# Rearranging K with VectorE block transposes in an attention backward for one query row: a new layout, new loads, a new order

## The chip, the cores and the metric

One core of a Trainium2 chip. The metric is the device time of one execution in microseconds (us). A run more than 1.5% above the fastest of its kernel is called slow and left out of comparisons. Ratios are the mean time of one kernel's fast runs over that of the other's of the same rounds on the same chip (the rounds ran on several chips, each with the kernel before beside the others), so they are not quite the ratio of the medians quoted beside them.

## The reference

```python
B, H, Sq, Skv, Dh = 1, 32, 1, 8192, 128           # bf16
def fwd(q, k, v):
    scores = einsum('bhqd,bhkd->bhqk', q, k) * Dh ** -0.5
    return einsum('bhqk,bhkd->bhqd', softmax(scores), v)
# returns (out, dq, dk, dv) for a given grad_out
```

For each of 32 heads one query row meets 8192 rows of K and V, 2.1 MB each. dK and dV are outer products, 2.1 MB each. So a head moves 8.39 MB and computes little on it: 268 MB in all.

## The kernel before

A head is two tiles of 128 partitions x 64 rows x 128 columns in SBUF, the on-chip memory that transfers write to; the tensor engine's results come out in another one, PSUM. The scores q.K and dp = dO.V contract over the columns, so the tensor engine (PE) transposes both tiles in 128x128 blocks, ScalarE (ACT) copies the result out of PSUM, and 64 narrow products (one column each) for K and 64 for V follow. VectorE (DVE) writes dK and dV as outer products. SyncE (SP) issues all transfers on one queue.

```python
def load(h):                                      # and load_v(h) the same
    Kt[h] = kvpool.tile([P, NT, D], BF16, tag="K", name="Kt")
    nc.sync.dma_start(Kt[h][:], k[0, h].rearrange("(p n) d -> p n d", p=P))
...
def transposes(h, which, c):                      # 4 of these for K, 4 for V
    T_ps = psT.tile([P, CH, P], BF16, tag="T", name="T_ps")
    for i in range(CH):                           # CH = 16
        nc.tensor.transpose(T_ps[:, i, :], Xt[:, c * CH + i, :], ident[:])
    nc.scalar.copy(X.rearrange("p c s -> p (c s)").bitcast(F32), ...)
...
def store(h, G, dst, part):                       # two stores of 1 MB for dK, two for dV
    nc.sync.dma_start(dst[0, h].rearrange("(p n) d -> p n d", p=P)[:, part * L:(part + 1) * L, :],
                      G[:, part * L:(part + 1) * L, :])
```

Of the kernel before, what the change touches and what calls it, by code (L numbers as in the profile page):

```python
# [8 lines left out]
ACT = mybir.ActivationFunctionType  # L9
ALU = mybir.AluOpType  # L10
AX = mybir.AxisListType
BF16 = mybir.dt.bfloat16
F32 = mybir.dt.float32
PSUM = bass.MemoryType.PSUM

CH = 16
R = 4
KV_BUFS = 3
AHEAD = 2
NST = 2  # L20


@with_exitstack
def kernel(
# [11 lines left out]
    nc = tc.nc  # L36
# [5 lines left out]
    assert NCH == 4  # L42
# [3 lines left out]
    kvpool = ctx.enter_context(tc.tile_pool(name="kv", bufs=KV_BUFS))  # L46
# [6 lines left out]
    Kt, Vt = {}, {}  # L53

    def load(h):
        Kt[h] = kvpool.tile([P, NT, D], BF16, tag="K", name="Kt")
        nc.sync.dma_start(Kt[h][:], k[0, h].rearrange("(p n) d -> p n d", p=P))

    def load_v(h):
        Vt[h] = kvpool.tile([P, NT, D], BF16, tag="V", name="Vt")  # L60
        nc.sync.dma_start(Vt[h][:], v[0, h].rearrange("(p n) d -> p n d", p=P))
# [4 lines left out]
    for h in range(AHEAD):  # L66
        load(h)
        load_v(h)
# [6 lines left out]
    nc.vector.memset(ones_f[:], 1.0)  # L75

    qT = consts.tile([P, H], BF16)
    doT = consts.tile([P, H], BF16)
    for i, colsT in ((0, qT), (1, doT)):
        tp = psT.tile([P, CH, P], BF16, tag="T")  # L80
        nc.tensor.transpose(tp[:, 0, 0:H], rows[:, i, :], ident[0:H, 0:H])
        nc.vector.tensor_copy(colsT[:], tp[:, 0, 0:H])

    o_allT = consts.tile([P, H], BF16)
    dq_allT = consts.tile([P, H], BF16)
# [4 lines left out]
    st = {}  # L90
    XT = {}

    def transposes(h, which, c):
        Xt = Kt[h] if which == "K" else Vt[h]
        T_ps = psT.tile([P, CH, P], BF16, tag="T", name="T_ps")
        for i in range(CH):
            nc.tensor.transpose(T_ps[:, i, :], Xt[:, c * CH + i, :], ident[:])  # L97
        X = tpool.tile([P, CH, P], BF16, tag="XT", name="XT_sb")
        nc.scalar.copy(X.rearrange("p c s -> p (c s)").bitcast(F32),  # L99
                       T_ps.rearrange("p c s -> p (c s)").bitcast(F32))  # L100
        XT[which, c] = X

    def scores(h, which, c):
        X = XT.pop((which, c))
        out_cols, vecT = (st[h]["s"], qT) if which == "K" else (st[h]["dp"], doT)
        for i in range(CH):
            n = c * CH + i
            nc.tensor.matmul(out_cols[:, n:n + 1], lhsT=X[:, i, :], rhs=vecT[:, h:h + 1],  # L108
                             start=True, stop=True, skip_group_check=True)

    def contract(Xt, rep, out_col):
        for n in range(NT):
            nc.tensor.matmul(out_col, lhsT=Xt[:, n, :], rhs=rep[:, n, 0:1],  # L113
                             start=(n == 0), stop=(n == NT - 1), skip_group_check=True)
# [8 lines left out]

    def store(h, G, dst, part):
        L = NT // NST
        nc.sync.dma_start(dst[0, h].rearrange("(p n) d -> p n d", p=P)[:, part * L:(part + 1) * L, :],
                            G[:, part * L:(part + 1) * L, :])

    def ds_of(h):
        x = st[h]  # L130
        nc.tensor.matmul(x["m"][:, 1:2], lhsT=ones_f[:], rhs=x["pd"][:], start=True, stop=True,  # L131
                         skip_group_check=True)
        pdt = small.tile([P, 1], F32, tag="pdt")
        nc.vector.tensor_copy(pdt[:], x["m"][:, 1:2])
        rep = small.tile([P, NT, R], BF16, tag="dsrep", name="ds_rep")
        nc.vector.scalar_tensor_tensor(
            out=rep[:], in0=x["dp"][:, 0:NT].unsqueeze(2).to_broadcast([P, NT, R]), scalar=pdt[:],
            in1=x["p_s"][:].unsqueeze(2).to_broadcast([P, NT, R]), op0=ALU.subtract, op1=ALU.mult)
        x["ds"] = rep

    def dq_of(h):
        x = st[h]
        contract(Kt[h], x["ds"], x["o"][:, 1:2])
        nc.scalar.copy(dq_allT[:, h:h + 1], x["o"][:, 1:2])  # L144

    def dk_outer(h):
        x = st[h]
        G = gpool.tile([P, NT, D], BF16, tag="g0", name="G0")
        for r in range(4):
            outer_part(G, x["ds"], x["qd"][:, 0, :], r)  # L150
            if r % (4 // NST) == 4 // NST - 1:
                store(h, G, out_2, r // (4 // NST))

    for h in range(H + 1):
        if h < H:
            x = st[h] = {}
            x["s"] = psS.tile([P, 512], F32, tag="s", name="s_ps")
            transposes(h, "K", 0)
        if h > 0:
            ds_of(h - 1)  # L160
        if h < H:
            transposes(h, "K", 1)
            scores(h, "K", 0)
            transposes(h, "K", 2)
        if h > 0:
            dq_of(h - 1)
            if h - 1 + KV_BUFS < H:
                load_v(h - 1 + KV_BUFS)
                load(h - 1 + KV_BUFS)
            dk_outer(h - 1)  # L170
        elif AHEAD < KV_BUFS:
            load(AHEAD)
            load_v(AHEAD)
        if h == H:
            break
        scores(h, "K", 1)
        transposes(h, "K", 3)
        scores(h, "K", 2)
        x["dp"] = psS.tile([P, 512], F32, tag="dp", name="dp_ps")
        transposes(h, "V", 0)  # L180
        scores(h, "K", 3)
        mx = small.tile([P, 1], F32, tag="mx")
        nc.vector.reduce_max(mx[:], x["s"][:, 0:NT], axis=AX.X)  # L183
        diag = small.tile([P, P], F32, tag="diag")
        nc.vector.tensor_scalar(diag[:], ident_f[:], mx[:], scale, op0=ALU.mult, op1=ALU.mult)
        transposes(h, "V", 1)
        x["m"] = psS.tile([P, 512], F32, tag="m", name="m_ps")
        nc.tensor.matmul(x["m"][:, 128:256], lhsT=ones_f[:], rhs=diag[:], start=True, stop=True,  # L188
                         skip_group_check=True)
        nbias = small.tile([P, 1], F32, tag="nbias")  # L190
        nc.vector.tensor_reduce(nbias[:], x["m"][:, 128:256], axis=AX.X, op=ALU.max, negate=True)  # L191
        e = small.tile([P, NT], F32, tag="e")
        rs = small.tile([P, 1], F32, tag="rs")
        nc.scalar.activation(e[:], x["s"][:, 0:NT], ACT.Exp, bias=nbias[:], scale=scale, accum_out=rs[:])
        scores(h, "V", 0)
        transposes(h, "V", 2)
        nc.tensor.matmul(x["m"][:, 0:1], lhsT=ones_f[:], rhs=rs[:], start=True, stop=True,  # L197
                         skip_group_check=True)
        rinv = small.tile([P, 1], F32, tag="rinv")
        nc.vector.reciprocal(rinv[:], x["m"][:, 0:1])  # L200
        p_rep = small.tile([P, NT, R], BF16, tag="prep")
        nc.scalar.activation(p_rep[:], e[:].unsqueeze(2).to_broadcast([P, NT, R]), ACT.Copy, scale=rinv[:])  # L202
        x["p_s"] = small.tile([P, NT], F32, tag="p_s", name="p_s")
        nc.vector.tensor_scalar(x["p_s"][:], e[:], rinv[:], scale, op0=ALU.mult, op1=ALU.mult)
        scores(h, "V", 1)
        transposes(h, "V", 3)
        nc.tensor.matmul(x["m"][:, 256:512], lhsT=ident[0:H, h:h + 1].to_broadcast([H, P]),  # L207
                         rhs=rows[:].rearrange("h a d -> h (a d)"), start=True, stop=True,
                         skip_group_check=True)
        qd = small.tile([P, 2, D], BF16, tag="qd")  # L210
        nc.scalar.copy(qd[:].rearrange("p a d -> p (a d)"), x["m"][:, 256:512])  # L211
        x["qd"] = qd
        scores(h, "V", 2)
        x["o"] = psS.tile([P, 512], F32, tag="o", name="o_ps")
        contract(Vt[h], p_rep, x["o"][:, 0:1])
        nc.scalar.copy(o_allT[:, h:h + 1], x["o"][:, 0:1])  # L216
        G = gpool.tile([P, NT, D], BF16, tag="g1", name="G1")
        for r in range(3):
            outer_part(G, p_rep, qd[:, 1, :], r)
            if r % (4 // NST) == 4 // NST - 1:  # L220
                store(h, G, out_3, r // (4 // NST))
        scores(h, "V", 3)
        junk = small.tile([P, NT], F32, tag="junk")
        pd = small.tile([P, 1], F32, tag="pd")
        nc.vector.tensor_tensor_reduce(out=junk[:], in0=x["p_s"][:], in1=x["dp"][:, 0:NT], scale=1.0 / scale,  # L225
                                       scalar=0.0, op0=ALU.mult, op1=ALU.add, accum_out=pd[:])
        x["pd"] = pd
        outer_part(G, p_rep, qd[:, 1, :], 3)
        store(h, G, out_3, NST - 1)

    order.__exit__(None, None, None)

    for srcT, dst in ((o_allT, out_0), (dq_allT, out_1)):
        fin_ps = psT.tile([P, CH, P], BF16, tag="T")
        nc.tensor.transpose(fin_ps[0:H, 0, :], srcT[:, 0:H], ident[:])
        fin_sb = small.tile([H, D], BF16, tag="fin")
        nc.vector.tensor_copy(fin_sb[:], fin_ps[0:H, 0, :])
        nc.sync.dma_start(dst.rearrange("b h s d -> (b h s) d"), fin_sb[:])
# [30 lines left out]
```

## Time and profile before

| | before |
|---|---|
| time, median of 4 | 668.09 us (667.35 to 672.16) |
| PE / DVE / ACT busy | 90% / 54% / 45% |
| the queue's packets, share of 16 DMA engines' time | 96.7% |
| traffic in the middle | 424 GB/s, 19.8 us a head |

How to read it: two figures are near 100%, PE's and the DMA engines'. A DMA engine is one of 16 units that move packets (a packet is here one contiguous run); the share is the time that their packets took.

### The profile page before, as it was taken

The numbers are of one execution on the slowest core, as the hardware profiler recorded it, in microseconds if no ns is written. First come the engines' busy times: TensorE is split into PE (matmuls) and PEld (weight loads), VectorE is DVE, ScalarE is ACT, GpSimd is POOL, SyncE is SP. The second block draws the span as 40 slices with busy tenths as digits, with TensorE's granted clock in tenths as the row PEclk, the third lists the DMA queues.
The fourth block names the chain that finished last, engine by engine and source line by source line (L and its number), as shares of the span: only waits on it lengthen the run. The fifth ranks groups of instructions, "written<-read, shape, count | busy, mean of one in ns | idle before, by whom it ended". The sixth has DMA issues, their size and how long they took to land.

```text
span 666.8 us, 26841 instructions
## 1 busy us (share of the span) xinstructions
PE 601.6 (90%) x12516; PEld 583.7 (88%) x12516; DVE 359.1 (54%) x550; ACT 302.5 (45%) x449; POOL 0.7 (0%) x6
## 2 busy tenths in 40 slices
PE   4999998998999999999999999998898999999991
PEld 4989998988998988998889998998888889999991
DVE  0644566545566654456644566545666544565444
ACT  2544434445544444444445434445444444444450
POOL 0000000000000000000000000000000000000000
PEclk9777658789877677656777657779777776567775
DMA  8999999999999999999999999999999999999746
GB/s 345 406 421 428 424 424 424 424 426 426 425 422 425 423 425 426 425 426 423 419 417 414 404 412 420 420 410 418 418 426 424 419 411 414 413 404 412 317 190 260
DMA packets 27951, 270.19 MB, mean 405 GB/s; under 512 B 3264, under 2 KB 3264, under 8 KB 3264
## 3 DMA queue, kind: packets, MB, share of 16 engines
q1 hardware_dynamic: 27840, 268.48, 96.7%
q8 instruction: 98, 1.61, 0.9%
q14 instruction: 13, 0.11, 0.0%
HBM read 134.23 MB, written 134.23 MB: 403 GB/s over the span
## 4 chain that ended last, share of the span: by engine, by line
PE 70%; DVE 10%; DMA 7%; issue 7%; ACT 4%; SPq 0%; DVEq 0%
PE T_ps L97 44%; PE o_ps L113 10%; DVE G L118 9%; PE s_ps L108 7%; PE dp_ps L108 5%; DMA Vt<-in_v_dram 5%; ACT XT_sb L99 3%; DMA Kt<-in_k_dram 3%; PE m_ps L131 2%; PE m_ps L188 1%; PE m_ps L197 1%; ACT qd L211 1%; DVE junk L225 0%; PE m_ps L207 0%; DVEq L264 0%
## 5 line engine op out<-in xcount | busy, mean ns | idle before, releaser
L99 ACT COPY XT_sb<-T_ps 128x1024 f32<-128x1024 f32 x256 | 259.1, 1012 | 282.3 <-PE T_ps L97 279.1
L97 PE MATMUL T_ps<-ident,Kt 128*128 128x128 bf16 x2048 | 214.6, 289 | 9.8 <-DMA Kt<-in_k_dram 6.3
L97 PEld LDWEIGHTS <-Kt 128*128 128x128 bf16 x2048 | 191.0, 136 | 10.9 <-DMA Kt<-in_k_dram 6.6
L118 DVE TENSOR_TENSOR G<-p_rep,qd 128x2048 bf16<-128x2048 bf16 x128 | 150.9, 1220 | 67.4 <-ACT qd L211 58.9
L97 PE MATMUL T_ps<-ident,Vt 128*128 128x128 bf16 x2048 | 168.2, 248 | 1.2 <-issue 1.2
L118 DVE TENSOR_TENSOR G<-ds_rep,qd 128x2048 bf16<-128x2048 bf16 x128 | 148.1, 1219 | 7.1 <-DMA out_dram<-G 6.2
L108 PEld LDWEIGHTS <-XT_sb 128*128 128x128 bf16 x4096 | 139.6, 101 | 9.7 <-issue 5.2
L97 PEld LDWEIGHTS <-Vt 128*128 128x128 bf16 x2048 | 146.2, 113 | 1.4 <-issue 1.4
L183 DVE TENSOR_REDUCE mx<-s_ps 128x1 f32<-128x64 f32 x32 | 7.2, 225 | 136.7 <-PE s_ps L108 136.7
L108 PE MATMUL s_ps<-qT,XT_sb 128*128 128x1 bf16 x2048 | 75.1, 166 | 0.0
L108 PE MATMUL dp_ps<-doT,XT_sb 128*128 128x1 bf16 x2048 | 70.6, 163 | 4.4 <-issue 4.4
L113 PE MATMUL o_ps<-p_rep,Vt 128*128 128x1 bf16 x2048 | 57.3, 163 | 8.0 <-issue 8.0
L113 PEld LDWEIGHTS <-Kt 128*128 128x128 bf16 x2048 | 59.8, 102 | 4.6 <-issue 4.6
L113 PE MATMUL o_ps<-ds_rep,Kt 128*128 128x1 bf16 x2048 | 59.7, 165 | 4.3 <-issue 3.0
L113 PEld LDWEIGHTS <-Vt 128*128 128x128 bf16 x2048 | 54.6, 96 | 8.6 <-issue 8.6
L131 PEld LDWEIGHTS m_ps<-pd,ones_f 128*128 128x128 f32 x64 | 16.4, 317 | 28.1 <-ACT XT_sb L99 18.4
L131 PE MATMUL m_ps<-pd,ones_f 128*128 128x1 f32 x64 | 17.5, 343 | 23.0 <-DVE pd L225 23.0
L200 DVE RECIPROCAL rinv<-m_ps 128x1 f32<-128x1 f32 x32 | 5.4, 168 | 43.1 <-PE m_ps L197 43.1
L191 DVE TENSOR_REDUCE nbias<-m_ps 128x1 f32<-128x128 f32 x32 | 9.3, 292 | 34.9 <-PE m_ps L188 34.9
L216 ACT CAST o_allT<-o_ps 128x1 bf16<-128x1 f32 x32 | 5.2, 162 | 42.0 <-PE o_ps L113 42.0
L144 ACT CAST dq_allT<-o_ps 128x1 bf16<-128x1 f32 x32 | 5.2, 162 | 27.7 <-PE o_ps L113 27.7
L202 ACT ACTIVATE p_rep<-e,rinv 128x256 bf16<-128x256 f32 x32 | 16.3, 511 | 0.0
(33 smaller groups left out, 138.0 us busy)
## 6 DMA issues: line engine op xcount, KB each, us to landing
out_dram<-G SPq DMA_DIRECT2D x128, 1024.0 KB, 22.9
Kt<-in_k_dram SPq DMA_DIRECT2D x32, 2048.0 KB, 25.6
Vt<-in_v_dram SPq DMA_DIRECT2D x32, 2048.0 KB, 25.4
out_dram<-fin_sb SPq DMA_DIRECT2D x2, 8.0 KB, 7.2
rows<-in_q_dram SPq DMA_DIRECT2D x1, 8.0 KB, 1.5
rows<-in_grad_out_dram SPq DMA_DIRECT2D x1, 8.0 KB, 1.8
```

The lines of the kernel that those rows point to most:

```text
L97: nc.tensor.transpose(T_ps[:, i, :], Xt[:, c * CH + i, :], ident[:])
L99: nc.scalar.copy(X.rearrange("p c s -> p (c s)").bitcast(F32), T_ps.rearrange("p c s -> p (c s)").bitcast(F32))
L108: nc.tensor.matmul(out_cols[:, n:n + 1], lhsT=X[:, i, :], rhs=vecT[:, h:h + 1], start=True, stop=True, skip_group_check=True)
L113: nc.tensor.matmul(out_col, lhsT=Xt[:, n, :], rhs=rep[:, n, 0:1], start=(n == 0), stop=(n == NT - 1), skip_group_check=True)
L118: nc.vector.tensor_tensor(G[:, r * Q:(r + 1) * Q, :].rearrange("p n (a b) -> p n a b", b=R), rep[:, r * Q:(r + 1) * Q, :].unsqueeze(2).to_ ...
L131: nc.tensor.matmul(x["m"][:, 1:2], lhsT=ones_f[:], rhs=x["pd"][:], start=True, stop=True, skip_group_check=True)
L183: nc.vector.reduce_max(mx[:], x["s"][:, 0:NT], axis=AX.X)
L188: nc.tensor.matmul(x["m"][:, 128:256], lhsT=ones_f[:], rhs=diag[:], start=True, stop=True, skip_group_check=True)
L191: nc.vector.tensor_reduce(nbias[:], x["m"][:, 128:256], axis=AX.X, op=ALU.max, negate=True)
L197: nc.tensor.matmul(x["m"][:, 0:1], lhsT=ones_f[:], rhs=rs[:], start=True, stop=True, skip_group_check=True)
L202: nc.scalar.activation(p_rep[:], e[:].unsqueeze(2).to_broadcast([P, NT, R]), ACT.Copy, scale=rinv[:])
L211: nc.scalar.copy(qd[:].rearrange("p a d -> p (a d)"), x["m"][:, 256:512])
```

## The change

Its intent: take the transposes of K off PE and ACT. DVE transposes K in 32x32 blocks of 4-byte words (two bf16 at a time), and PE multiplies the blocks with a q spread block-diagonally (each group of 32 partitions meets its own column), so that the scores come out in the layout that V already has. For that K must lie in SBUF in another order of rows, and ds, the gradient of the scores, must be permuted for dQ. The sum over p*dp becomes O.dO. Loads are issued ahead of stores, K before V.

```diff
-KV_BUFS = 3
+K_BUFS = 3
+V_BUFS = 2
-        nc.sync.dma_start(Kt[h][:], k[0, h].rearrange("(p n) d -> p n d", p=P))
+        rows_of = k[0, h].rearrange("(n i a g) d -> n a i (g d)", n=NCH, i=QD, a=NQ)   # 4, 32, 4
+        for n in range(NCH):
+            nc.sync.dma_start(Kt[h][:, n * CH:(n + 1) * CH, :].rearrange("p g d -> p (g d)"), rows_of[n])
...
+            nc.vector.transpose(XK[h][:, :, :, n, :],
+                                Kt[h][:, part, :].rearrange("p g d -> p (g d)").bitcast(F32).rearrange(
+                                    "p (g w j) -> p g w j", g=CH, w=NB))
...
+        for g in range(CH):
+            for c in range(2 * NB):
+                nc.tensor.matmul(out[:, g, :], lhsT=cols[:, g, c // 2, c % 2], rhs=q_blk[:, h, c, :],
+                                 start=(c == 0), stop=(c == 2 * NB - 1), skip_group_check=True)
...
-        nc.vector.tensor_tensor_reduce(out=junk[:], in0=x["p_s"][:], in1=x["dp"][:, 0:NT], ...)
+        nc.tensor.matmul(x["m"][:, 1:2], lhsT=do_f[:, h:h + 1].to_broadcast([P, P]), rhs=o_all[:, h:h + 1],
+                         start=True, stop=True, skip_group_check=True)
```

(Cut: the mask and the permutation of ds, the order of the loop, the four-part first and last transfers.)

## The prediction

> **What bounds the kernel now.** I read the page's busy row first, then the sliced rows, then a table by stretches, then the issues of transfers and their landing, and only then the groups of instructions.
>
> ```profile
> PE 601.6 (90%) x12516; PEld 583.7 (88%) x12516; DVE 359.1 (54%) x550; ACT 302.5 (45%) x449; POOL 0.7 (0%) x6
> ...
> DMA  8999999999999999999999999999999999999746
> GB/s 345 406 421 428 424 424 424 424 426 426 425 422 425 423 425 426 425 426 423 419 417 414 404 412 420 420 410 418 418 426 424 419 411 414 413 404 412 317 190 260
> ...
> q1 hardware_dynamic: 27840, 268.48, 96.7%
> ```
>
> The tensor engine is busy for 90%, and the chain that ended last is 70% of its work, but the transfers are as full: the row GB/s stands flat at 404 to 428 over thirty-five of forty slices, whatever the engines do, and the queue's packets fill 96.7% of 16 engines' time. The stretches say it more sharply (columns: stretch, its length, busy PE, PEld, DVE, ACT, POOL, granted clock, share of the 16 DMA engines, GB/s):
>
> ```profile
> 133.00:333.00 200.00, 185.66 (x3975) 180.54 (x3974) 114.27 (x173) 95.16 (x141) 0.00 (x0) 0.74 1.01 424
> ...
> 634.00:667.00 33.00, 18.00 (x407) 17.20 (x405) 15.93 (x23) 8.00 (x14) 0.00 (x0) 0.60 0.55 221
> ```
>
> In the middle the share is 1.01: no DMA engine is ever free. One head is 8.39 MB (2.1 each of K in, V in, dK out, dV out); at 424 GB/s that is 19.8 us, and 268.48 MB at 424 is 633 us of the span's 666.8. The other 34 us are the start (first slice 345 GB/s) and above all the last 65 us, which move less. So the kernel is bound by its 16 DMA engines, with PE close behind (18.6 us of 20 a head in the middle), and each engine moves 424/16 = 26.5 GB/s. The packet records behind these rows give the pace of one engine: nearly every packet of 8192 bytes (stores) took 309 ns, of 16384 bytes (loads) 611 ns, so 302 ns per 8 KB plus about 7.
>
> ```profile
> out_dram<-G SPq DMA_DIRECT2D x128, 1024.0 KB, 22.9
> Kt<-in_k_dram SPq DMA_DIRECT2D x32, 2048.0 KB, 25.6
> Vt<-in_v_dram SPq DMA_DIRECT2D x32, 2048.0 KB, 25.4
> ...
> L99 ACT COPY XT_sb<-T_ps 128x1024 f32<-128x1024 f32 x256 | 259.1, 1012 | 282.3 <-PE T_ps L97 279.1
> L97 PE MATMUL T_ps<-ident,Kt 128*128 128x128 bf16 x2048 | 214.6, 289 | 9.8 <-DMA Kt<-in_k_dram 6.3 <-issue 3.4
> L118 DVE TENSOR_TENSOR G<-p_rep,qd 128x2048 bf16<-128x2048 bf16 x128 | 150.9, 1220 | 67.4 <-ACT qd L211 58.9 <-DMA Vt<-in_v_dram 6.3 <-DMA Kt<-in_k_dram 2.1
> ```
>
> A transfer lands 23 to 26 us after issue, about 10 MB at 424 GB/s: the queue is always deep. K's transposes are 214.6 us of PE time, the largest thing the change removes, but PE is not the first limit.
>
> [...]
>
> **The change, part by part.**
>
> *How K is loaded.* This is the part I take to decide. The source pattern changes from (p n) d with p = 128 slowest to "n a i (g d)": each of four transfers a head has the source dimensions a = 4, i = 32, then a run of 16 rows of 256 bytes, 4096 bytes. The steps of a (16 rows) and i (64 rows) don't merge, so the built instruction carries 4 as its slowest source dimension, against 128 partitions at the destination. [...]
>
> Work of one of those four engines for a head: K is 4 transfers x 32 packets of 4096 bytes; by the pace above a packet is 151 + 7 = 158 ns (estimate), so 128 x 158 = 20.2 us. Its sixteenth of V is 8 packets x 611 = 4.9 us. Its sixteenth of the four 1 MB stores is 4 x 8 x 309 = 9.9 us. Sum 35.0 us, against 4.9 + 4.9 + 9.9 = 19.7 before. The other twelve have 14.8 us of work and then wait. One queue is used[...], and a head is finished when the slowest engine is. 32 x 35.0 = 1120 us, with about 3 us ahead of the first packet and 10 us behind the last products as now: 1133 us, mean traffic 268.5/1133 = 237 GB/s.
>
> Can the queue run dry and add to it? At most eight transfers are in flight, by the semaphores of the built program; a head has nine. When K of head h+1 lands, K of h+2, dV of h and V of h+2 are already queued, 20.2 + 4.9 + 4.9 = 30 us for these engines, and dK of h comes about 10 us later, so no.
>
> [...]
>
> *What leaves PE and ACT.* 64 transposes a head, 214.6/32 = 6.7 us of PE, and half of 256 evictions at 1012 ns, 4.0 us of ACT a head. The reduction of p*dp (6.8 + 2.6 us on DVE in all) and the matmul for it go; one f32 matmul of dO with O takes their place. All of that lies beside transfers and gains nothing on the end.
>
> *What DVE takes on.* 128 block transposes of 1024 four-byte elements. [...]they are like the 128x2048 bf16 product[...], 1220 ns in the trace, so 1.2 us each (estimate), 156 us in all; 32 masked copies of ds at about 0.4 us are 13. DVE goes from 359 to about 359 - 9 + 169 = 519 us, 16.2 us a head. PE gets 2048 score products four columns wide in the place of as many one wide, and 128 small ones that permute ds: under 1 us a head. PE falls to some 12 us a head. Both fit under 35.
>
> *Order.* Loads ahead of stores and finer first and last transfers would save part of the 34 us at the ends: at most 15 us, against a loss of some 470.
>
> **The rivals.**
>
> *All 16 engines after all.* [...]a K packet of 4096 bytes costs 158 ns and a head 32 x 158 + 14.8 = 19.9 us: traffic as before, PE no longer near the limit, better ends, about 645 us (-3.5%). For it: the care spent on the ends looks like work on a kernel near its traffic limit. [...]
>
> *16 engines, DVE bound.* The products (8 x 1.22), the transposes (4 x 1.22) and the rest are 16.2 us a head in one ordered stream, which waits for PE and ACT at the softmax statistics about three times a head, some 1 to 2 us each: near 20 us a head, 650 to 680 us, the same as now. It needs the first rival to hold.
>
> [...]
>
> **Range and chances.** I give four engines 80%. [...]I put the middle at 1160, skewed upward. A range that also held 645 would say nothing, so mine lies on one side: 1090[...] to 1560. Of the other 20%, faster has 0.12 (first rival), the same 0.06, slower the rest.
>
> **What would show it.** Right: in the profile after, GB/s near 235 with a DMA share near 0.6 in the middle, K's transfers landing tens of us after issue, PE, DVE and ACT idle mostly for K's landing (the block transposes as the group that waits), a period of 35 us a head, and packets of 4096 bytes at 158 ns. [...] Wrong: a share near 1.0 and 420 GB/s in the middle with a period of 20 us, or idle time of DVE ended by PE instead of by K.

What no trace or run of this case shows is cut from the prediction, and the cuts are marked. They took out the ground for four engines, a term of the sum with the rival that belonged to it, and the ground of the lower end, 1090. That the new source pattern puts K's transfers on four engines was the assumption; the runs below show it (3424 small packets, a share of 0.25). The sum that stands comes to 32 x 35.0 + 13 = 1133 us. The middle, 1160, and the upper end, 1560, held the cut term besides: packets of K at up to twice their 158 ns, which would be up to 40.4 us of K a head and (40.4 + 14.8) x 32 = 1766 us (estimate). That a block transpose takes as long as the product of 2048 bf16 columns, 1220 ns in the trace before, was an estimate too; in the changed kernel it takes 1239.

## The result

The changed kernel takes 1231.52 us (median of 4, 1230.09 to 1232.17) against 668.09: a ratio of 1.841, 95% interval 1.833 to 1.848. Results are right.

The page of the changed kernel: busy time by engine, the DMA share and GB/s in 40 slices, the packet counts, the queue.

```profile
PE 484.5 (39%) x10599; PEld 464.5 (38%) x10599; DVE 519.8 (42%) x678; ACT 179.5 (15%) x353; POOL 0.7 (0%) x6
...
DMA  4476557765577655766546665466654566545676
GB/s 130 144 246 209 202 192 248 249 205 212 188 249 251 224 197 185 250 254 239 195 197 234 253 250 188 188 224 251 253 204 190 207 251 248 207 191 196 252 270 260
DMA packets 41665, 269.96 MB, mean 220 GB/s; under 512 B 3424, under 2 KB 3424, under 8 KB 21856
...
q1 hardware_dynamic: 41568, 268.48, 59.7%
```

The same bytes move at half the pace, and no engine is busy even half of the time. The count of packets under 512 bytes is worth working out. The sum comes out if a transfer ends with one small packet (4 bytes in the packet records) from each DMA engine that took part; the four transfers of q, grad_out, out and dq add 4 x 32 = 128 packets of 256 bytes. The changed kernel issues 302 transfers. On 16 engines each that would be 302 x 16 + 128 = 4960. With 174 transfers on 16 and K's 128 on 4 it is 2784 + 512 + 128 = 3424, which is the number in the line. (The same sum for the kernel before: 196 x 16 + 128 = 3264, also its number.)

The stretches of the changed kernel (columns: stretch, length, busy PE, PEld, DVE, ACT, POOL, granted clock, DMA share, GB/s), chosen over two heads:

```profile
606.00:622.00 16.00, 0.96 (x23) 0.88 (x19) 5.76 (x6) 0.16 (x1) 0.00 (x0) 0.50 1.01 374
624.00:642.00 18.00, 10.32 (x185) 9.71 (x183) 5.51 (x9) 3.83 (x8) 0.00 (x0) 0.50 0.26 101
644.00:660.00 16.00, 2.50 (x80) 2.42 (x77) 7.70 (x7) 0.75 (x2) 0.00 (x0) 0.50 1.00 374
662.00:680.00 18.00, 9.97 (x168) 9.37 (x165) 5.00 (x9) 3.99 (x9) 0.00 (x0) 0.50 0.25 100
```

The DMA engines alternate between all busy and a quarter busy: in 18 of 38 us a share of 0.25 is four engines of 16, and 101 GB/s is 25 from each. The mean share of 0.6 hides that. The packet records say the same: from 50 us to 40 us before the last packet exactly four packets were in flight for 46% of the time, and 15 to 17 for 44%.

The groups of the changed kernel (busy, mean ns of one, then idle time before them and what ended it):

```profile
L147 PE MATMUL T_ps<-ident,Vt 128*128 128x128 bf16 x2048 | 216.4, 296 | 214.0 <-DMA Vt<-in_v_dram 214.0
L130 DVE STREAM_TRANSPOSE XK_sb<-Kt 128x1024 f32<-128x1024 f32 x128 | 157.5, 1239 | 330.2 <-DMA Kt<-in_k_dram 329.8
...
L141 PE MATMUL s_ps<-q_blk,XK_sb 128*128 128x4 bf16 x2048 | 59.8, 168 | 498.4 <-DVE pdt L197 488.6
```

DVE waits 330 us for K, PE 214 us for V, which stands behind K in the same queue. PE's longest wait, 489 us before the score products, is for a small DVE copy (pdt); in DVE's order that copy stands behind the next head's block transposes, so this too is K's landing at one remove. The block transposes themselves take 1239 ns.

The chain that ended last, by engine, of the kernel before:

```profile
PE 70%; DVE 10%; DMA 7%; issue 7%; ACT 4%; SPq 0%; DVEq 0%
```

and of the changed kernel, with its first issues (size, and where a landing time would stand):

```profile
DMA 66%; PE 25%; DVE 4%; SPq 2%; ACT 1%; issue 1%; ACTq 0%
...
Kt<-in_k_dram SPq DMA_DIRECT2D x128, 512.0 KB
out_dram<-G_dv SPq DMA_DIRECT2D x62, 1024.0 KB
```

The chain has gone from PE to the transfers (64% of the span V's, which wait behind K, and 2% K's own). The page prints no landing time any more, because it pairs every transfer with 16 completion events. The kept trace has them: on each of its eight semaphores (the counters that tell of landings) the events add up with 16 for every other transfer and 5 for each of K's, four from the engines if the small packets are read rightly, and one more. Counted so, K lands a median of 31 us after issue, the tens of us that the prediction had named as a sign.

The starts of the first block transpose of each head, read from the trace, give the period: 37.1 to 40.3 us in the steady part, mean 38. 32 x 38.0 + 13 is 1229, the span.

### The profile page after: what moved, and what is told of

Read it like the earlier page. It is cut to its first block, busy times and chain, and to the rows that moved or that the text cites. A ratio compares the mean times of both kernels' runs of the same rounds, so it can differ in the third digit from the quotient of the medians.

```text
span 1229.5 us, 22993 instructions
## 1 busy us (share of the span) xinstructions
PE 484.5 (39%) x10599; PEld 464.5 (38%) x10599; DVE 519.8 (42%) x678; ACT 179.5 (15%) x353; POOL 0.7 (0%) x6
## 2 busy tenths in 40 slices
DMA packets 41665, 269.96 MB, mean 220 GB/s; under 512 B 3424, under 2 KB 3424, under 8 KB 21856
## 4 chain that ended last, share of the span: by engine, by line
DMA 66%; PE 25%; DVE 4%; SPq 2%; ACT 1%; issue 1%; ACTq 0%
DMA Vt<-in_v_dram 64%; PE T_ps L147 14%; PE o_ps L162 6%; DVE G_dv L167 3%; PE dp_ps L157 3%; DMA Kt<-in_k_dram 2%; PE m_ps L237 1%; SPq L183 1%; SPq L66 1%; PE m_ps L188 1%; ACT p_rep L264 1%; ACT XT_sb L149 0%; PE m_ps L258 0%; DVE G_dk L167 0%; PE m_ps L273 0%
## 5 line engine op out<-in xcount | busy, mean ns | idle before, releaser
L130 DVE STREAM_TRANSPOSE XK_sb<-Kt 128x1024 f32<-128x1024 f32 x128 | 157.5, 1239 | 330.2 <-DMA Kt<-in_k_dram 329.8
L147 PEld LDWEIGHTS <-Vt 128*128 128x128 bf16 x2048 | 194.4, 138 | 218.9 <-DMA Vt<-in_v_dram 218.9
L141 PE MATMUL s_ps<-q_blk,XK_sb 128*128 128x4 bf16 x2048 | 59.8, 168 | 498.4 <-DVE pdt L197 488.6
L141 PEld LDWEIGHTS <-XK_sb 128*128 128x128 bf16 x2048 | 57.1, 104 | 501.4 <-DVE pdt L197 491.2
L149 ACT COPY XT_sb<-T_ps 128x1024 f32<-128x1024 f32 x128 | 129.6, 1012 | 376.1 <-PE T_ps L147 376.1
L167 DVE TENSOR_TENSOR G_dv<-p_rep,qd 128x2048 bf16<-128x2048 bf16 x128 | 148.2, 1220 | 21.9 <-ACT p_rep L264 21.2
L167 DVE TENSOR_TENSOR G_dk<-ds_rep,qd 128x2048 bf16<-128x2048 bf16 x128 | 153.0, 1216 | 0.0
L157 PEld LDWEIGHTS <-XT_sb 128*128 128x128 bf16 x2048 | 72.4, 106 | 5.6 <-issue 3.9
L162 PE MATMUL o_ps<-dsk,Kt 128*128 128x1 bf16 x2048 | 57.0, 164 | 0.3 <-ACT dsk L216 0.3
L162 PEld LDWEIGHTS <-Vt 128*128 128x128 bf16 x2048 | 56.9, 103 | 0.0
L162 PEld LDWEIGHTS <-Kt 128*128 128x128 bf16 x2048 | 55.0, 99 | 0.4 <-issue 0.4
```

The source lines that it names most:

```text
L130: nc.vector.transpose(XK[h][:, :, :, n, :], Kt[h][:, part, :].rearrange("p g d -> p (g d)").bitcast(F32).rearrange("p (g w j) -> p g w j", ...
L141: nc.tensor.matmul(out[:, g, :], lhsT=cols[:, g, c // 2, c % 2], rhs=q_blk[:, h, c, :], start=(c == 0), stop=(c == 2 * NB - 1), skip_group ...
L147: nc.tensor.transpose(T_ps[:, i, :], Vt[h][:, c * CH + i, :], ident[:])
L157: nc.tensor.matmul(st[h]["dp"][:, n:n + 1], lhsT=X[:, i, :], rhs=doT[:, h:h + 1], start=True, stop=True, skip_group_check=True)
L162: nc.tensor.matmul(out_col, lhsT=Xt[:, n, :], rhs=cols[:, n, 0:1], start=(n == 0), stop=(n == NT - 1), skip_group_check=True)
L167: nc.vector.tensor_tensor(G[:, r * Q:(r + 1) * Q, :].rearrange("p n (a b) -> p n a b", b=R), rep[:, r * Q:(r + 1) * Q, :].unsqueeze(2).to_ ...
```

## Experiments

Eleven kernels ran; their diffs are cut to the lines that matter. The first four separate the causes, the next three look at stretched packets and at a repair, the last four look at what the rest of the change is worth.

### k_quadrants: the changed kernel, K's transfers cut the other way

```diff
-        rows_of = k[0, h].rearrange("(n i a g) d -> n a i (g d)", n=NCH, i=QD, a=NQ)
-        for n in range(NCH):
-            nc.sync.dma_start(Kt[h][:, n * CH:(n + 1) * CH, :].rearrange("p g d -> p (g d)"), rows_of[n])
+        rows_of = k[0, h].rearrange("(n i a g) d -> a i n (g d)", n=NCH, i=QD, a=NQ)
+        for a in range(NQ):
+            nc.sync.dma_start(Kt[h][a * QD:(a + 1) * QD].rearrange("p (n g) d -> p n (g d)", n=NCH), rows_of[a])
```

> The changed kernel with K loaded by four transfers of one quadrant each (32 partitions slowest on both sides), same 4096-byte runs, same bytes, same places, all else as in the changed kernel. Theory (four DMA engines carry K): now 16 engines, 8 packets an engine and transfer, so K is 32 x 159 ns = 5.1 us a head and the head 19.9 us: about 650 us. [...] The small packets in the trace become 302 transfers x 16 + 128 = 4960 (3424 in the changed kernel). Rival A (runs of 4096 bytes and many small transfers are slow): stays near 1230. Rival B (the new DVE and PE chain sets the period of 38 us): stays near 1230.

866.33 us (862.65 to 874.75), ratio 1.295 (1.286 to 1.304); right. The same bytes in the same runs to the same places, and 365 us are gone. The page's lines on transfers, and the middle of the run as one stretch:

```profile
DMA  8999999999999999999999999999999999999985
GB/s 230 254 362 363 356 339 350 371 364 346 336 316 342 299 299 297 318 333 278 307 292 332 313 299 296 305 337 288 303 297 322 337 284 307 293 330 318 275 340 215
DMA packets 43202, 269.97 MB, mean 314 GB/s; under 512 B 4960, under 2 KB 4960, under 8 KB 23392
...
133.00:800.00 667.00, 372.47 (x8181) 357.43 (x8178) 389.69 (x492) 137.93 (x273) 0.00 (x0) 0.55 0.99 316
```

4960 small packets: 16 engines each. Rivals A and B fall: runs of 4096 bytes and the new chain of instructions are both still there. But the share is 0.99 at only 316 GB/s: the packets are stretched. Half of those of 4096 bytes took 319 ns or more, twice the 159 of an undisturbed one. The expectation had a second sum for that, 318 ns a packet, 10.2 us of K and 25.0 us a head, about 810 us (an estimate); 866 is 7% above it and far from the 650 expected with packets at 159 ns. What stretches them is not shown.

### before_k4: the kernel before, with K's pattern alone

```diff
-        nc.sync.dma_start(Kt[h][:], k[0, h].rearrange("(p n) d -> p n d", p=P))
+        nc.sync.dma_start(Kt[h].rearrange("p n d -> p (n d)"), k[0, h].rearrange("(i a n) d -> a i (n d)", i=32, a=4))
```

> The kernel before, with nothing changed but K's source pattern, (i a n) d with a = 4 slowest and i = 32 inside it, runs of 16384 bytes kept; results wrong on purpose (K's rows are permuted against V's). Theory: four engines take 32 packets x 611 ns = 19.6 us of K a head + 14.8 us of the rest = 34.4 us: 32 x 34.4 + 13 = 1114 us, up to about 1210 if the same 3 us a head are lost as in the changed kernel. Rival A (small runs): 668. Rival B (DVE and PE chain): 668.

1273.72 us (1266.71 to 1282.95), ratio 1.904 (1.890 to 1.919). Its output is wrong, which doesn't matter for the time. One line of the kernel before, one transfer a head in the same runs of 16384 bytes, and the whole loss is there; it is 64 us more than the 1210 at the upper edge of what was expected.

```profile
DMA packets 27567, 270.19 MB, mean 213 GB/s; under 512 B 2880, under 2 KB 2880, under 8 KB 2880
```

164 x 16 + 32 x 4 + 128 = 2880: four engines. The head takes (1273.7 - 13)/32 = 39.4 us against 34.4 worked out; the sum misses 5 us here. after_no_v below looks at such a loss in the changed kernel; for this one it stays open.

### before_k4kb: small runs on 16 engines

```diff
-        nc.sync.dma_start(Kt[h][:], k[0, h].rearrange("(p n) d -> p n d", p=P))
+        for n in range(NCH):
+            nc.sync.dma_start(Kt[h][:, n * CH:(n + 1) * CH, :],
+                              k[0, h].rearrange("(p n) d -> p n d", p=P)[:, n * CH:(n + 1) * CH, :])
```

> The kernel before with K loaded in four transfers of 512 KB, runs of 4096 bytes, 128 partitions slowest. Theory: 16 engines as before, K 32 x 159 ns = 5.1 us an engine instead of 4.9, so 20.0 us a head: 668 to 680 us, within 2%. Rival A (runs of 4096 bytes and transfers of 512 KB are slow): over 800.

672.83 us (671.68 to 676.47), ratio 1.005 (1.000 to 1.010), as expected. Four transfers of 512 KB in runs of 4096 bytes cost 0.5%, at the edge of the noise; rival A is out by itself too.

### after_no_v: where the other 3 us a head come from

```diff
     def load_v(h):
-        Vt[h] = vpool.tile([P, NT, D], BF16, tag="V", name="Vt")
+        if h >= 2:
+            Vt[h] = v_kept[h % 2]
+            return
+        Vt[h] = v_kept[h % 2] = vpool.tile([P, NT, D], BF16, tag="V", name="Vt")
```

> The changed kernel with V loaded for the first two heads only and those two tiles used in turn; results wrong on purpose. For the 38.0 us a head measured against 35.0 predicted. Theory (packets of K meet packets of V[...] and both slow down): without V nearly every 4096-byte packet takes 159 ns (in the changed kernel a fifth of them take 165 to 350), a head is 128 x 159 + 9.9 = 30.2 us: about 980 us. Rival C[...]: the 3 us stay, 33 us a head, about 1070.

984.55 us (983.36 to 985.60), ratio 1.469 (1.463 to 1.476). Its output is wrong, which doesn't matter for the time. Its page:

```profile
GB/s 134 145 150 197 234 235 234 191 168 217 235 235 235 169 174 235 234 233 204 167 207 234 235 234 175 168 234 235 234 209 168 200 235 235 235 189 159 229 311 270
DMA packets 36912, 207.03 MB, mean 211 GB/s; under 512 B 2896, under 2 KB 2896, under 8 KB 20816
```

A quarter fewer bytes at the same low traffic: K's four engines still set the pace. The sum without V, 30.2 us a head, now fits to 5 us in the whole run. So with V in the stream, packets slowed down; without it hardly any (4096 bytes: 177 ns on average without the first and last 100 us, against 160 without V). In the packet records of the changed kernel (100 to 900 us) the 4096-byte packets fall into three kinds: when at most five packets were in flight they took 164 ns on average; when all engines were busy mostly with stores, 163; when all were busy and at least ten packets were loads, 265, and the 16384-byte packets of V beside them 884 instead of 611. K's packets are not slowed by each other, nor by stores, but beside V's. Where on their way from HBM, the large memory that K and V come from, into SBUF the two hold each other up is not shown: the records don't name the engine of a packet.

### before_halves: 64 partitions a transfer

```diff
-        nc.sync.dma_start(Kt[h][:], k[0, h].rearrange("(p n) d -> p n d", p=P))
+        for half in (0, 64):
+            nc.sync.dma_start(Kt[h][half:half + 64],
+                              k[0, h].rearrange("(p n) d -> p n d", p=P)[half:half + 64])
```

> The kernel before with K loaded by two transfers of 64 partitions (0-63, 64-127), 16 engines each, runs of 16384 bytes kept, results right. [...] Theory[...]: K's packets take up to 1222 ns instead of 611, K 9.8 us a head instead of 4.9, the head 24.6 us: about 800 us, at least 730. Rival (what counts is only how many engines carry a transfer, or its source pattern): 668 to 680.

828.37 us median of 4 (821.23 to 843.07), of which two count as slow; the two fast ones, 821.23 and 822.76, are 1.23 times the 669 of the kernel before. Results are right. Each transfer has 16 engines (3776 small packets are 228 x 16 + 128), and the packets say what happened: of those of 16384 bytes (K's and V's) a quarter stayed at 611 ns and a quarter took 1201 or more; the middle one took 842. The page again shows a full share with low traffic:

```profile
DMA  8999999999999999999999999999999999999985
GB/s 243 259 354 359 299 295 337 366 360 301 358 268 315 332 291 298 333 337 340 312 292 332 321 308 332 306 380 350 356 359 370 356 342 357 378 352 377 369 332 239
```

So the stretching is not a matter of how many engines take part. The 153 us that are lost are 4.8 a head, so K takes about 9.7 us instead of 4.9 (estimate): in transfers of 64 neighbouring partitions K came at about half of the pace that it has in transfers of 128. The runs that are read are the same as before, only in two halves; what holds the packets up is not shown.

### k_quad_2q: quadrants 0 and 1 from SP, 2 and 3 from ACT

```diff
-        for a in range(NQ):
-            nc.sync.dma_start(...)             # arguments cut, the same on both sides
+        for a, queue in ((0, nc.sync), (2, nc.scalar), (1, nc.sync), (3, nc.scalar)):
+            queue.dma_start(...)
```

> The kernel of k_quadrants with quadrants 0 and 1 issued from SP and quadrants 2 and 3 from ACT[...]. Theory[...] K between 5.1 and 10.2 us a head, so faster than the 866 of k_quadrants, 700 to 820; the waits that now stand in ACT's stream may take some of it back. Rival (32-partition transfers are slow[...]): 866 or more.

816.81 us (812.14 to 831.06), ratio 1.219 (1.215 to 1.223), the upper edge of what was expected. Its profile fell in the slow state (831.06 us), so only the timed runs count. The idea was that packets for partitions 0 to 63 and for 64 to 127 are then in flight together; whether they were is not shown. It is faster than 866, as expected, but ACT's stream now holds waits, and how much of a larger gain they took back is not shown.

### all16: another layout, 16 engines everywhere

The rows are laid out so that K keeps runs of 16384 bytes and V and the stores become (a p g) with 128 partitions slowest and runs of 4096 bytes; the block transposes then have to write four chunks interleaved.

```diff
-        rows_of = v[0, h].rearrange("(p n) d -> p n d", p=P)
+        rows_of = v[0, h].rearrange("(a p g) d -> p a (g d)", a=NQ, p=P)
-            nc.vector.transpose(XK[h][:, :, :, n, :],
+            nc.vector.transpose(XK[h][:, :, :, :, n],
```

> The changed kernel with the rows laid out so that every transfer has 128 partitions slowest: K as in the kernel before (runs of 16384 bytes), V and the stores as (a p g) with runs of 4096 bytes; the block transposes write four chunks interleaved, the masks follow; results right. Theory: 16 engines everywhere[...]: K 8 x 611 + V 32 x 159 + stores 64 x 159 ns = 20.2 us a head, 645 + 13 = about 658 us, a little faster than the kernel before (0.98 to 0.99), with PE near 65%. Rival B (the chain of DVE and PE, 16.2 us busy on DVE with waits at the softmax): over 670 with a DMA share clearly under 1.

774.62 us (768.82 to 776.35), ratio 1.156 (1.152 to 1.161); right, but not the 658 expected. (The diff leaves out K's load, the stores, which change as V does, and the masks.) This line of its groups tells why:

```profile
L133 DVE STREAM_TRANSPOSE XK_sb<-Kt 128x1024 f32<-128x1024 f32 x128 | 236.1, 1959 | 4.7 <-DMA Kt<-in_k_dram 4.7
```

Writing with a step of four words made the transpose 1959 ns instead of 1239. DVE hardly waits for K any more (4.7 us in all): rival B of this run holds, DVE's stream is the bound, and the DMA share between 133 and 733 us is 0.94.

### all16_perm: transposes written together, the scores permuted

```diff
-            nc.vector.transpose(XK[h][:, :, :, :, n],
+            nc.vector.transpose(XK[h][:, :, :, n, :],
+        nc.scalar.copy(s_sb[:], x["s"][:, 0:NT])
+        nc.tensor.matmul(x["s"][:, 128:128 + NT], lhsT=perm_f[:].rearrange("p i n -> p (i n)"), rhs=s_sb[:],
+                         start=True, stop=True, skip_group_check=True)
```

> The kernel of all16 with the block transposes writing each chunk together again and the rows of the scores put in order by one f32 permutation product a head (one ACT copy of 128x64 more); results right. all16 ran at 774.6 with its transposes at 1959 ns (1239 in the changed kernel) and DVE at 18.6 us busy in 23.8 a head. If the interleaved write is what made them slow, they return to 1239 ns: 4 x 0.72 = 2.9 us less a head, 20.9 us, about 682 us. If all16 was held by its transfers, it stays near 770.

702.29 us (702.05 to 702.96), ratio 1.049 (1.046 to 1.051); right.

```profile
DMA packets 56768, 269.95 MB, mean 385 GB/s; under 512 B 3424, under 2 KB 3424, under 8 KB 52576
...
q1 hardware_dynamic: 56672, 268.48, 97.8%
...
L136 DVE STREAM_TRANSPOSE XK_sb<-Kt 128x1024 f32<-128x1024 f32 x128 | 147.7, 1212 | 4.3 <-DMA Kt<-in_k_dram 4.3
```

The 3424 small packets are 206 x 16 + 128, so every transfer has 16 engines. The transposes are back at 1212 ns, so the step of the write was the cause, and the 72 us that this saves show that DVE's stream had held all16. The time is 20 us above the 682 expected; the extra copy and product lie in the chain to the maximum, and I have not separated their share.

### all16_fill: two of the transposes into DVE's gaps

```diff
-K_BUFS = 3
+K_BUFS = 4
-        if h + 2 < H:
-            load_k(h + 2)
+        if h + 1 < H:
+            k_blocks(h + 1, (0, 1))          # two of four; the other two stay where they were
+        if h + 3 < H:
+            load_k(h + 3)
```

> The kernel of all16_perm with four buffers for K, K loaded one head earlier, and two of the next head's four block transposes put into the DVE stream where it waits for the softmax sum. In all16 DVE waits about 2.1 us a head for the maximum and 2.1 us for the sum. If DVE's stream is the bound of all16_perm, some 2 us a head go and the transfers (20.2 us a head) bind: 655 to 665 us, 0.98 to 0.995 of the kernel before. If not, the time of all16_perm.

676.12 us (674.11 to 676.53), ratio 1.009 (1.007 to 1.011); right. Filling the gaps, the fourth buffer and the earlier load together took 26 us away. That DVE's order had been the bound of all16_perm is not shown by it: three things changed at once, and the DMA engines of all16_perm were hardly idle (a share of 97.8%, 1.01 between 133 and 600 us at 396 GB/s). Its packets took longer: 164 ns on average for 4096 bytes and 703 for 16384, against 161 and 658 here, which is 96 x 3 + 8 x 45 = 650 ns an engine and head, some 21 of the 26 us (estimate). What had stretched them is open. Now the transfers bind, and runs of 4096 bytes for three quarters of the bytes make them slower than in the kernel before: by the packets' pace 20.2 us a head instead of 19.7, as in the expectation. The time missed its range by some 11 us.

### natural: the change's arithmetic with the old transfers

The permutation is applied to the scores in both partition and column (a masked f32 copy and four f32 products), so that K, V and the stores can all keep the layout of the kernel before, and ds needs none.

```diff
-        rows_of = k[0, h].rearrange("(n i a g) d -> n a i (g d)", n=NCH, i=QD, a=NQ)
+        rows_of = k[0, h].rearrange("(p n) d -> p n d", p=P)
+    def s_swap(h):
+        for a in range(NQ):
+            nc.tensor.matmul(x["s"][:, 128:128 + NT], lhsT=swap_w[:, a, :],
+                             rhs=x["sm"][:, a].rearrange("p n g -> p (n g)"),
+                             start=(a == 0), stop=(a == NQ - 1), skip_group_check=True)
...
-            contract(Kt.pop(p_), st[p_]["dsk"], ...)
+            contract(Kt.pop(p_), st[p_]["ds"], ...)
```

> The changed kernel's arithmetic with every transfer as in the kernel before (K and V in runs of 16384 bytes, stores of 8192, 128 partitions slowest): the permutation is applied to the scores (one masked f32 copy and four f32 products a head) and no longer to ds, order of DVE as in all16_fill; results right. Theory: the transfers bind at K 4.9 + V 4.9 + stores 9.9 = 19.7 us a head with a share of 1.0, so 631 + 13 to 20 us at the ends: 644 to 655 us, 0.965 to 0.98 of the kernel before. Rival (DVE's ordered stream or PE, now with more f32 products, binds): 668 or more, with a share under 1.0 in the middle.

667.51 us (664.69 to 669.68), ratio 0.996 (0.991 to 1.000); right. The same time as before, and not the 644 to 655 expected. The page and the stretches of this kernel:

```profile
PE 535.2 (80%) x10727; PEld 518.6 (78%) x10727; DVE 514.0 (77%) x679; ACT 172.8 (26%) x321; POOL 0.7 (0%) x6
...
133.00:533.00 400.00, 336.00 (x6628) 325.50 (x6626) 313.72 (x396) 107.15 (x200) 0.00 (x0) 0.53 1.01 420
600.00:634.00 34.00, 29.60 (x603) 28.95 (x600) 25.01 (x33) 10.72 (x20) 0.00 (x0) 0.60 0.84 330
634.00:667.00 33.00, 20.11 (x404) 19.13 (x403) 20.38 (x30) 5.52 (x11) 0.00 (x0) 0.50 0.65 258
```

In the same middle stretch the kernel before has:

```profile
133.00:533.00 400.00, 371.22 (x7848) 360.78 (x7847) 224.57 (x342) 188.53 (x281) 0.00 (x0) 0.73 1.01 420
```

PE has 35 us less to do in these 400, and the traffic is the same 420 GB/s at a full share. All of PE's relief lay beside the transfers. At the end both run thin: 330 and 258 GB/s here, 364 and 221 in the kernel before.

### natural_lead2: K two heads ahead instead of three

```diff
-K_BUFS = 4
+K_BUFS = 3
-        if h + 3 < H:
-            load_k(h + 3)
+        if h + 2 < H:
+            load_k(h + 2)
```

> The kernel natural with K loaded two heads ahead and three buffers, not three ahead and four. In natural the last load lands at 609 of 667 us and after it only stores are left, at 258 GB/s in the last 33 us. If loads that run ahead of the stores are what leaves this thin end, one K load (2.1 MB, 4.9 us) moves out of it into the full middle: about 662 us (0.99 of the kernel before). If the earlier landing of K is needed by the DVE stream, the block transposes wait for K and the time is 670 or more.

676.97 us (671.66 to 680.21), ratio 1.011 (1.006 to 1.015); right. By time and by sign the second of the two: DVE now waits for K.

```profile
133.00:533.00 400.00, 329.16 (x6610) 320.08 (x6608) 309.83 (x391) 105.82 (x197) 0.00 (x0) 0.56 1.01 413
600.00:634.00 34.00, 24.42 (x506) 23.95 (x502) 27.53 (x35) 6.75 (x13) 0.00 (x0) 0.61 0.99 391
...
DVE XK_sb L135 <- DMA Kt<-in_k_dram: 40.5, 15, 3.4
```

(The last line is of the waits: us in total, times, longest; in natural the same wait is 2.6 us, once.) But the DMA engines did not go idle for it: the share is 1.01 in the middle, at 413 GB/s instead of 420. The packets again took longer, 645 ns for 16384 bytes and 318 for 8192 against 630 and 314 in natural: 16 x 15 + 32 x 4 = 370 ns an engine and head, 12 us in all (estimate), about the whole loss. So that the wait for K is what cost the time is not shown. The load did move towards the end, where 391 GB/s flow between 600 and 634 us instead of 330, but what that is worth is covered by the loss before it. (The expectation also misread the trace: 609 us is where natural's last K lands; the last quarter of its last V lands at 636.) No version beat the kernel before by more than the noise.

## Why the prediction was right

*Direction and mechanism: right.* The step it called decisive was the source pattern: 4 as the slowest dimension, so four DMA engines. The changed kernel shows 3424 small packets and stretches with a share of 0.25; before_k4 puts that pattern alone into the kernel before and finds 1273.72 us; k_quadrants takes it alone out and finds 866.33. This is shown, not only argued, and the packets' own pace (164 ns with four at work) says that it is the number of engines and not a slow pattern. What the runs show is the counts of small packets: with 4 as the slowest dimension of the source they give 4 engines (3424 in the changed kernel, 2880 in before_k4), with 32 (k_quadrants, 4960), 64 (before_halves, 3776) and 128 (the kernel before, 3264) they give 16.

*Pace of a packet: right.* 158 ns was worked out for 4096 bytes; the median is 159.

*The head's sum: too small, mostly by one term.* 35.0 us a head were worked out and 38.0 measured, 1133 us against 1231.52. The term that was mis-sized is K, 128 x 158 ns = 20.2. Without the first and last 100 us, where V and the stores have small packets too, the mean of the 4096-byte packets is 177 ns, and 128 x 177 = 22.6 us: 2.4 of the missing 3.0. The stores' packets, 331 ns on average instead of 309, would make the rest, 32 x 22 ns = 0.7, if K's four engines have their share of that (estimate). after_no_v shows whose doing it is: V's.

*Slow packets: right that they cost, wrong about which.* In the term that is cut, K's packets slowed each other. They didn't: with at most five packets in flight they took 164 ns on average. K's packets are slow beside those of V, 265 ns. The text had put only the chance of the first kind into the upper end of its range; the measured 1231.52 lies inside it, 6% above the middle, so that the range held it is partly luck: the room was there for a slowing that did not happen.

*The queue never dry: right.* Between 50 us and 40 us before the last packet, fewer than four packets were in flight for under 2% of the time.

*DVE: right, part by part.* 519 us predicted, 519.8 measured; block transposes 156 us predicted and 157.5 measured (1239 ns each), masked copies 13 and 13.6. The comparison with the bf16 product can be worked out from the trace before: a maximum over 128 f32 columns takes 292 ns and one over 64 225, so about 1.05 ns a column and 158 ns besides, while the product of 2048 bf16 columns takes 1220 ns, at most 0.60 a column. 1024 words at 1.05 ns and 158 are 1.23 us (estimate). *PE: too small.* 12 us a head were predicted, 484.5/32 = 15.1 measured. V's transposes alone took 296 ns each, against 248 before, together 48 us more and half of what was missed; the granted clock was 0.55 instead of 0.72. It cost nothing, as PE waits.

*Small slips.* The row GB/s stands at 404 to 428 over thirty-six slices, not thirty-five. Of the signs that were to show it, the share (0.60), the traffic (220 GB/s, 235 named) and DVE's wait for K came; PE and ACT wait for K only at one remove.

*The rivals.* All 16 engines after all: not so, but natural tests what it promised, 645 us for the change with 16 engines, and finds 667.51. The error there is the ends, which were to be better and are not: the span is still some 34 us above 633. DVE bound at 650 to 680 us: all16 shows that DVE's ordered stream binds when its transposes are slow; all16_fill at 676.12 lies in the range and all16_perm at 702.29 above it, but in both the transfers are full as well.

*Open:* why before_k4 loses 5 us a head where the changed kernel loses 3; which part of k_quad_2q's time is ACT's waits; what stretches K's packets beside V's, and the packets of k_quadrants, before_halves, all16_perm and natural_lead2; and what would fill the last 65 us.

## What to carry to other kernels

Before rearranging a load, look at the slowest dimension of its source pattern and at the partitions that one transfer covers: a source pattern with 4 in front made the kernel 84% longer here, and 90% in before_k4, where bytes, run length and the destination tile were as before; transfers of 64 partitions instead of 128 made it 23% longer (before_halves). Read traffic and DMA share together: here a low share at low traffic (0.26 at 101 GB/s) meant that too few engines had work, and a full share at low traffic (0.99 at 316) meant stretched packets. And ask what the removed work stood beside: with the old transfers, taking K's transposes off PE changed the time by 0.4%, within the noise.
